# Two of four batches mixed as one 2x2 block product of seven products, with feature-major outputs

## The chip, the cores and the metric

The kernel runs on one core of one Trainium2 chip. The metric is the device time of one execution, in microseconds (us). Three runs of the kernel before took 250.44, 250.61 and 252.2 us; the median is 250.61. A profiled execution is a run of its own, whose span the views of the trace show.

## The reference

Polynomial-sketch attention for 4 batches of 4 heads, 1088 positions and 32 features a head, followed by a token-mixing block whose two 1088x1088 weight matrices are shared by all batches. The parts that matter here:

```
phi(x) = outer(S1 x, S2 x)                    # 8 x 8 sketch features
kv  = sum_s phi(k) v ;  z = sum_s phi(k)
x   = (phi(q) kv) / (phi(q) z + 1e-6)         # (4, 4, 1088, 32) -> (4, 1088, 128)
theta = x @ w_theta
zr, zi = x * cos(theta), x * sin(theta)
y   = einsum('ts,bsd->btd', w_tok_r, zr) + einsum('ts,bsd->btd', w_tok_i, zi)
u   = x + y
out = u + relu(u @ w_ch)                      # (4, 1088, 128), float32
```

The inputs `w_tok_r`, `w_tok_i`, `w_theta`, `w_ch`, `S1` and `S2` arrive as 64-bit floats and are turned into 32-bit floats by the kernel.

## The kernel before

The kernel is a list of operations, each recorded with its engine, an assumed duration, the buffers that it reads and writes, and a due time. The class `Layout` lays them out: a list scheduler with a duration model (`dve`, `act`, `pool_`, `LAT`) plays the engines forward and takes at each step the operation with the lowest rank; ranks come from due times, and the table `SHIFT` moves each stage's rank by a hand-held number. The order that comes out is what is issued on each engine (`issue`), and semaphores are set by the tile framework. Where the model sees a gap on TensorE in the first part, `issue` puts filler matmuls (`spin`, L432). Buffers come from pools by class: 22 of `big` (1152 floats a partition), 5 of `zs`, 6 of `g1`, 8 PSUM banks `ps`, and so on. Helpers issue nearly everything, so many groups of the profile share a line: `tt` is L380 (tensor_tensor, on DVE or POOL, and a custom DVE addition too), `ts` L384, `stt` L387, `mm` L400, and `join` L394 is a DMA issued by POOL that adds its source to its destination.

The stages, in their rough order of time:

- Keys and values of batch 0 are loaded and k is transposed (L789), sketched and summed into `kv`; then batch 1; then batches 2 and 3 together (`CHAINS`). q is loaded for each batch (L667 issues these loads on SP), transposed, and made into the levels `lv`.
- The mixing weights arrive as 17 rows of 1088 64-bit numbers a partition (`w_tok` into `zs`): 8 chunks of 128 source positions for the real matrix, 8 for the imaginary one, and one that holds the last 64 positions of both. A 64-bit row becomes a 32-bit one with two ACT operations (L651, L653), a DVE shift (L384) and a custom DVE addition (L380); it stays in a `big` buffer, `rows[i]`, with 128 source positions on partitions and 1088 target positions along the free axis.
- `outputs_x(b)` makes, in three groups of 384 positions, the attention's output `xT[b]` with features on partitions (ACT copy), theta, its cosine and sine, and `zt[b]`: 17 chunks of 128 positions by 128 features, the chunks of `x cos` first, then those of `x sin`, and the mixed one of 64 + 64.
- `mix_row(b, i, ...)` multiplies chunk i of `zt[b]` (standing, 128x128) with row i (moving, 384, 384 and 320 columns). 17 of these add up in PSUM to y of the batch, with features on partitions. Batch 0 does its three groups of columns together, row by row as the rows arrive; the later batches do one group after another. Batch 3 has other cuts (`LAST`: 320, 384, 256 and 128 columns), so that the last group is short.
- `mix_out(b, span, yp)` finishes a group of columns. For batches 0 and 1 (`UDMA`, `ODMA`), ACT copies y out of PSUM, and a `join` adds x; then for each 128 positions a matmul gives u @ w_ch with positions on partitions (u standing), a transpose gives u itself (L1168), ACT applies relu (L1183) and copies u (L1189), a second `join` adds them. For batches 2 and 3 both additions are DVE operations (L380) that read PSUM. The store (L1195, on SP) writes 512-byte rows.

All weight rows are kept until the end, since every batch needs them.

Of the kernel before, what the change touches and what calls it, by code (L numbers as in the profile page):

```python
# [22 lines left out]
P = 128  # L23
# [11 lines left out]
    "blocks_k": 73.9, "blocks_m": 29.8, "blocks_t": -262.8, "chain0": -12.2, "chain1": -7.3, "chain2": 57.8,  # L35
    "den0": -124.6, "den1": -153.1, "den2": 103.7, "den3": 241.9, "first": -48.4, "grid0": -93.7, "grid1": 2.6,
    "grid2": -78.4, "grid3": 13.5, "kT0": -128.1, "kT1": -103.7, "kT2": -37.4, "kT3": -24.2, "keys0": -394.4,
    "keys1": -128.6, "keys2": -52.3, "keys3": -193.5, "kf0": -216.8, "kf1": 19.7, "kf2": -83.1, "kf3": -91.6,
    "kv0": -174.5, "kv1": 35.5, "kv2": 8.3, "kv3": -25.5, "kvb0": 0.1, "kvb1": -229.1, "kvb2": 126.9,
    "levels0": -99.2, "levels1": -206.9, "levels2": 66.3, "levels3": 253.2, "loadh1": -83.9, "loadh2": -39.6,  # L40
    "loadh3": -67.9, "loadk0": 62.2, "loadk1": -58.1, "loadk2": -68.8, "loadk3": -79.3, "loadq0": -44.5,
    "loadq1": -58.0, "loadq2": -25.3, "loadq3": 17.3, "loadv0": -23.7, "loadv1": -50.2, "loadv2": -36.8,
    "loadv3": -35.8, "mix0_0": 247.6, "mix1_0": 81.4, "mix1_1": 70.9, "mix1_2": 137.9, "mix2_0": 319.4,
    "mix2_1": 370.4, "mix2_2": 512.5, "mix3_0": 275.2, "mix3_1": 124.7, "mix3_2": 81.7, "mix3_3": 52.5,
    "num0_0": -23.5, "num0_1": -122.6, "num0_2": -2.3, "num1_0": -980.1, "num1_1": -572.2, "num1_2": -805.8,
    "num2_0": 92.7, "num2_1": 137.9, "num2_2": 336.8, "num3_0": 216.9, "num3_1": 198.2, "num3_2": 256.2,
    "out0_0": 119.7, "out0_1": 79.8, "out0_2": 119.8, "out1_0": 206.2, "out1_1": 67.6, "out1_2": 380.5,
    "out2_0": 219.3, "out2_1": 329.6, "out2_2": 151.1, "out3_0": 206.6, "out3_1": 598.8, "out3_2": 247.9,
    "out3_3": 65.4, "q00": -178.0, "q01": -9.8, "q02": 44.9, "q03": 187.8, "qT0": -24.9, "qT1": 80.4, "qT2": 33.8,
    "qT3": 94.6, "qscale0": -72.3, "qscale1": 1.7, "qscale2": -12.0, "qscale3": 148.3, "rest0": -152.2,  # L50
    "rest1": -19.2, "rest2": 49.7, "rest3": -17.9, "row0": -3.7, "row1": -2.9, "row10": 57.0, "row11": 37.7,
    "row12": 37.2, "row13": 55.0, "row14": 73.7, "row15": 77.2, "row16": 66.5, "row2": 8.2, "row3": 28.3,
    "row4": 28.5, "row5": 29.4, "row6": 32.2, "row7": 33.8, "row8": 56.5, "row9": 60.6, "scaled": -81.5,
    "sliced": 215.7, "small": -186.7, "square2": -114.8, "sums0": -154.7, "sums1": -29.3, "sums2": 301.1,
    "sums3": -87.5, "theta0_0": -468.7, "theta0_1": -402.8, "theta0_2": -418.4, "theta1_0": -695.8,
    "theta1_1": -466.0, "theta1_2": -397.2, "theta2_0": 97.6, "theta2_1": 129.7, "theta2_2": 231.5,
    "theta3_0": 395.1, "theta3_1": 390.2, "theta3_2": 276.6, "w2": -38.6,
# [9 lines left out]
LAST = (0, 320, 704, 960)  # L67
# [4 lines left out]
ODMA = (True, True, False, False)  # L72
# [21 lines left out]
class Layout:  # L94
# [4 lines left out]
    LAT = {"P": 0.16, "V": 0.12, "A": 0.12, "G": 0.16, "S": 0.10}  # L99
# [58 lines left out]
    def lag(self, o, t):  # L158
        return o.fly + (0.0 if o.eng == t.eng else self.LAT[o.eng])

# [9 lines left out]
    def forward(self):  # L170
# [7 lines left out]
        channel = 0.0  # L178
# [51 lines left out]
        while done < len(ops):  # L230
# [12 lines left out]
            if e == "S":  # L243
                free[e] = t + self.ISSUE * max(o.lk, 1)
                channel = max(channel, free[e]) + o.dur
                o.end = channel + 2.0
            else:
                d = o.dur
                if e == "V" and o.lk > 1 and port["G"][1] > t - 0.3:
                    d += 0.25 * o.lk  # L250
                free[e] = t + d
                o.end = t + d + o.fly
                if o.lk and e in "VG":
                    port[e] = (t, t + d, o.lk)
# [9 lines left out]
            for s in o.succ:  # L264
                x = ops[s]
                x.wait -= 1
                x.ready = max(x.ready, o.end + (0.0 if x.eng == e else self.LAT[e]))
# [51 lines left out]
def kernel(  # L319
# [24 lines left out]
    GW = GC * P  # L344

# [46 lines left out]
    def join(dst, src, w, r, fly=ADD_FLY):  # L392

        op("G", 0.7, lambda: G.dma_start(dst(), src(), accum_op=ALU.add), w, r, fly=fly)  # L394
# [140 lines left out]
    op("G", 0.6, rests, [sf, sq], [sc, s0], lk=3)  # L535
# [61 lines left out]
    op("G", 1.9, lambda: blocks_m(0), [(mv[0], "s"), (mf[0], "s")], [s0, c16, cf, hm], lk=8)  # L597
# [233 lines left out]
    def chain(bs):  # L831
# [91 lines left out]
        op("G", 0.5 * nb, whole, [(mf[b], "y") for b in bs], [w_[1]] + [(mv[b], "y") for b in bs], lk=2 * nb)  # L923
        nus[bs] = nu

    def chain_out(bs):
        nu = nus[bs]
        at("kvb", bs[0])
        for n, b in enumerate(bs):
# [7 lines left out]
            op("G", 0.4, masks, [(mk, 0)], [bdm, nu, ec], lk=2)  # L937
# [7 lines left out]
            op("G", 0.6, eps, [(mk, 1), (qsb, 1)], [nu, (qsb, 0), ec], lk=3)  # L945
# [9 lines left out]
    qs, qx, q0, xT, zt = {}, {}, {}, {}, {}  # L955

# [95 lines left out]
    def outputs_x(b, lv, pool_qp):  # L1052
# [3 lines left out]
        for g in range(NG):  # L1056
# [32 lines left out]
            op("A", act(GW), lambda g=g, xp=xp: A.copy(xt()[:, g * GW:(g + 1) * GW], xp()), [(xt, g)], [xp])  # L1089
# [3 lines left out]
            cs = buf("g3", (2, GC, P), F32, "cs")  # L1093

            def turn(g=g, x=x, th=th):
                for i in range(GC):
                    y_ = xt()[:, g * GW + i * P:g * GW + (i + 1) * P]
                    T.transpose(x()[:, i], y_, ident())  # L1098

            def theta(g=g, th=th):  # L1100
# [4 lines left out]
            op("P", 0.67, theta, [th], [(xt, g), w2], hold=[cs])  # L1105
            op("P", 0.33, turn, [x], [(xt, g)])
# [12 lines left out]
                bc(x()[:, 0:full], 1, [P, 2, full, P]), cs()[:, :, 0:full], ALU.mult), [(z, g)], [x, cs])  # L1119
# [6 lines left out]


    rows = []

    def zkey(i):  # L1130
        return NG if i == NK - 1 else (i % NF) // GC

    def mix_row(b, i, gs, yps, due):
# [8 lines left out]
        op("P", w * 4 / 2400 + 0.01, f, yps, [(z, zkey(i)), rows[i]], due)  # L1142

    def mix_out(b, span, yp, due):
# [4 lines left out]
        xkeys = [(xt, j) for j in range(t0 // GW, (t1 - 1) // GW + 1)]  # L1149
        uT = buf("g1", (GW,), F32, "uT")  # L1150
        if UDMA[b]:
            op("A", act(w), lambda: A.copy(uT()[:, :w], yp()[:, :w]), [uT], [yp])
            join(lambda: uT()[:, :w], lambda: xt()[:, t0:t1], [uT], xkeys, ADD_FLY2)
        else:
            vop(w, lambda: tt(V, uT()[:, :w], xt()[:, t0:t1], yp()[:, :w], ALU.add), [uT], xkeys + [yp])
        po, un = buf("ps", (GW,), F32, "po"), buf("ps", (GW,), F32, "un")
        ot = buf("g1", (GC, DM), F32, "ot")
        nch = (w + P - 1) // P

        def lin():  # L1160
            for i in range(nch):
                sz = min(P, w - i * P)
                mm(po()[:sz, i * P:(i + 1) * P], uT()[:, i * P:i * P + sz], w2()[:, 1], True, True)

        def back():
            for i in range(nch):
                sz = min(P, w - i * P)
                T.transpose(un()[:sz, i * P:(i + 1) * P], uT()[:, i * P:i * P + sz], ident())  # L1168
# [121 lines left out]
```

## Time and profile before

| what | value |
|---|---|
| runs | 250.44, 250.61, 252.2 us (median 250.61) |
| span of the profiled execution | 248.5 us, 3915 instructions |
| TensorE (PE) busy | 239.7 us, 96%, 1480 matmuls |
| VectorE (DVE) busy | 142.1 us, 57%, 295 instructions |
| ScalarE (ACT) busy | 127.8 us, 51%, 255 |
| GpSimd (POOL) busy | 41.2 us, 17%, 96 |
| DMA | 34.54 MB in 11,922 packets, 139 GB/s on average; 2.23 MB of it written |
| granted TensorE clock | full, but for 0.94 of it in the stretch from 40 to 60 us |
| first product step of batch 0 (`mix_row`) | 63.67 us |

The profiled execution's span stands 2.1 us under the median of the runs. In the page's list of groups, each row names line, engine, operation, tiles and shapes, then the busy time of the group and the mean of one in ns, and at the end the idle time of the engine just before these instructions and what ended it. A matmul of 32-bit floats leaves two matmul records, and each record is about as long as its pipeline, longer than the distance between two starts; so a step is read as the distance from one start to the next. In a timeline, neighbouring instructions of one kind are drawn together, with their count behind the x.

### The profile page before, as it was taken

The page shows a single profiled execution, that of the slowest core. Times are in us where ns is not written, and L with a number is a line of the kernel's source. Part 1 is how long each engine was busy: PE and PEld are TensorE (multiplying, and loading weights), DVE is VectorE, ACT ScalarE, POOL GpSimd, SP SyncE. Part 2 cuts the span into 40 slices and gives each one's busy share as a digit, 9 for nine tenths or more (in the row PEclk, how much of TensorE's full clock was granted, in tenths as well). Part 3 has the DMA queues.
Part 4 walks back from the last instruction along what each step waited for, and adds up shares of the span by engine and source line. Part 5 has one row for each costly group of instructions (what it writes and reads, how often), then busy time and mean ns, then how long its engine had stood idle before and what let it go on. Part 6 is the DMA issues. An engine that isn't in the chain of part 4 may idle for free.

```text
span 248.5 us, 3915 instructions
## 1 busy us (share of the span) xinstructions
PE 239.7 (96%) x1480; PEld 178.6 (72%) x1480; DVE 142.1 (57%) x295; ACT 127.8 (51%) x255; POOL 41.2 (17%) x96
## 2 busy tenths in 40 slices
PE   7898999988999999999999999999999999999993
PEld 4797999958665766865766777696646679856773
DVE  2767898889988899999578101448802350100022
ACT  3787787589797998870433425674243360000011
POOL 1259441020000100007302332412000000000000
PEclk9999999997999999999999999999999999999999
DMA  6999999602470359991003255431101010000012
GB/s 204 372 417 338 423 369 427 282 0 95 154 291 3 96 175 356 370 396 57 3 0 63 63 92 127 79 66 24 30 0 34 0 32 3 0 11 0 0 47 59
DMA packets 11922, 34.54 MB, mean 139 GB/s; under 512 B 1280, under 2 KB 7296, under 8 KB 9728
## 3 DMA queue, kind: packets, MB, share of 16 engines
q1 hardware_dynamic: 9488, 30.29, 32.4%
q0 software_dynamic: 2320, 4.00, 8.2%
q8 instruction: 11, 0.18, 0.3%
q14 instruction: 7, 0.06, 0.1%
q10 hardware_dynamic: 96, 0.01, 0.0%
HBM read 28.07 MB, written 2.23 MB: 122 GB/s over the span
## 4 chain that ended last, share of the span: by engine, by line
PE 84%; DMA 11%; ACT 3%; SPq 0%; DVE 0%; issue 0%; DVEq 0%; ACTq 0%
PE ps L400 76%; DMA zs<-w_tok 6%; DMA big<-k_l 5%; PE ps L1076 3%; PE ps L1168 2%; PE ps L1098 2%; PE ps L987 1%; ACT big L651 0%; SPq L667 0%; ACT big L653 0%; PE ps L789 0%; ACT g L1111 0%; DVE g L387 0%; ACT g L1110 0%; ACT g L1107 0%
## 5 line engine op out<-in xcount | busy, mean ns | idle before, releaser
L400 PE MATMUL ps<-big,zs 128*128 128x384 f32 (+3 forms) x442 | 132.0, 447 | 0.0
L400 PEld LDWEIGHTS ps<-big,zs 128*128 128x128 f32 x442 | 78.2, 190 | 37.7 <-issue 2.6
L380 DVE CUSTOM_DVE_ANT_0 big<-big,big 128x2176 uint16<-128x2176 uint16 x17 | 21.9, 1291 | 3.4 <-ACT big L653 2.3
L651 ACT ACTIVATE big<-zs 128x1088 f32<-128x1088 f32 x17 | 20.7, 1219 | 4.8 <-DMA zs<-w_tok 4.8
L653 ACT ACTIVATE big<-zs 128x1088 int32<-128x1088 uint32 (+1 forms) x18 | 21.2, 1179 | 0.0
L380 DVE TENSOR_TENSOR g<-big,ps 128x384 f32<-128x384 f32 (+3 forms) x7 | 3.3, 478 | 26.8 <-PE ps L400 26.7
L1179 ACT COPY g<-ps 128x128 f32<-128x128 f32 (+1 forms) x2 | 0.6, 320 | 32.8 <-PE ps L1168 32.8
L1080 ACT COPY g<-ps 128x384 f32<-128x384 f32 x24 | 11.0, 487 | 11.1 <-PE ps L1076 11.0
L380 DVE TENSOR_TENSOR zs<-ps,g 128x768 f32<-128x768 f32 (+2 forms) x20 | 12.1, 627 | 7.4 <-ACT g L1113 5.7
L400 PE MATMUL ps<-mf,big 128*128 128x96 f32 x72 | 15.5, 313 | 0.0
L1183 ACT ACTIVATE g<-ps 128x384 f32<-128x384 f32 (+2 forms) x15 | 5.6, 401 | 18.7 <-PE ps L400 13.5
L387 DVE SCALAR_TENSOR_TENSOR g<-g,ps 128x384 f32<-128x384 f32 x12 | 6.6, 552 | 14.8 <-ACT g L1107 14.7
L384 DVE TENSOR_SCALAR big<-big 128x1088 int32<-128x1088 int32 x17 | 12.2, 719 | 1.8 <-ACT big L651 1.8
L400 PEld LDWEIGHTS <-hf 128*128 128x128 f16 (+1 forms) x144 | 11.9, 110 | 1.7 <-issue 1.3
L1020 ACT COPY lv<-ps 128x480 f32<-128x480 f32 x12 | 6.4, 578 | 12.3 <-PE ps L400 12.2
L400 PEld LDWEIGHTS ps<-w,big 128*128 128x128 f32 x72 | 9.3, 191 | 3.7 <-ACT big L1089 2.0
L400 PEld LDWEIGHTS ps<-mf,big 128*128 128x128 f32 x72 | 11.8, 207 | 0.0
L400 PE MATMUL ps<-w,big 128*128 128x128 f32 x72 | 10.0, 278 | 1.8 <-ACT big L1089 1.8
L380 DVE TENSOR_TENSOR g<-lv 128x768 f32<-128x768 f32 x12 | 11.1, 953 | 1.0 <-PE ps L1076 0.9
L1076 PEld LDWEIGHTS ps<-ident,g 128*128 128x128 f32 x72 | 8.7, 142 | 4.1 <-issue 1.3
L400 PE MATMUL ps<-mv,hf 128*128 128x96 f16 x108 | 11.2, 215 | 0.0
L1076 PE MATMUL ps<-ident,g 128*128 128x128 f32 x72 | 10.9, 275 | 0.0
(177 smaller groups left out, 371.5 us busy)
## 6 DMA issues: line engine op xcount, KB each, us to landing
zs<-w_tok SPq DMA_DIRECT2D x17, 1088.0 KB, 7.3
big<-k_l SPq DMA_DIRECT2D x7, 576.0 KB, 7.0
big<-q_l SPq DMA_DIRECT2D x4, 576.0 KB, 7.6
big<-v_l SPq DMA_DIRECT2D x4, 576.0 KB, 10.4
big<-hf POOLq DMA_DIRECT2D x3, 576.0 KB, 9.3
out<-g SPq DMA_DIRECT2D x7, 192.0 KB, 2.0
g<-big POOLq DMA_DIRECT2D x4, 192.0 KB, 2.9
g<-g POOLq DMA_DIRECT2D x4, 192.0 KB, 3.2
```

What stands on the lines that cost most here:

```text
L380: eng.tensor_tensor(out=o, in0=a, in1=b, op=f)
L384: (eng or V).tensor_scalar(out=o, in0=a, scalar1=s1, scalar2=s2, op0=op0, **kw)
L387: (eng or V).scalar_tensor_tensor(out=o, in0=a, scalar=s, in1=b, op0=op0, op1=op1)
L400: T.matmul(o, lhs, rhs, start=start, stop=stop, skip_group_check=True)
L651: op("A", 0.22 + n * 0.0009, lambda: A.activation(dfn(), words_of(raw(), n)[1].bitcast(F32), AF.Prelu, scale=2.0**-112, alpha=-(2.0**32)), ...
L653: op("A", 0.22 + n * 0.0009, lambda: A.activation(stp(), words_of(raw(), n)[0].bitcast(U32), AF.Copy, scale=2.0**-29), [stp], [raw])
L1020: op("A", act(480), lambda g=g, lp=lp: A.copy(lv().rearrange("p l (c n) -> p l c n", n=HR)[:, :, g * GC:(g + 1) * GC], lp().rearrange("p c ...
L1076: T.transpose(tr()[:, i * P:(i + 1) * P], qp()[:, i * H + 2 * n:i * H + 2 * n + 2].rearrange("p h i j -> p (h i j)"), ident())
L1080: op("A", act(GW), lambda n=n, tr=tr, qT=qT: A.copy(qT()[:, n], tr()), [(qT, n)], [tr])
L1098: T.transpose(x()[:, i], y_, ident())
L1168: T.transpose(un()[:sz, i * P:(i + 1) * P], uT()[:, i * P:i * P + sz], ident())
L1183: op("A", act(m), lambda n=n, i0=i0, i1=i1, o=o: A.activation(o(), po()[:n, i0 * P:i1 * P], AF.Relu), [(ot, j)], [po])
```

## The change

Batches 2 and 3 (`PAIR`) no longer run through `mix_row`. The two are one product: a 2x2 block matrix of z (rows: batch p = 2 and q = 3; columns: the 8 chunks of `x cos` and the 8 of `x sin`) times a 2x2 block matrix of weights (rows: real and imaginary; columns: the first and the second 544 target positions, `HT`). With a11 and a12 the first 544 columns of the real and of the imaginary rows, and a21 and a22 their second 544, `winograd` computes it in the variant of Strassen's algorithm with seven products in place of eight: each has 8 chunks and 544 columns, in two parts of 288 and 256 (`PARTS`). The sums of weights are made in place on the halves of the rows, "1" and "2" on DVE, "4" and "3" on POOL (`APOOL`); the sums of z (`zsub`) on DVE. Products accumulate on one another in PSUM where a later result contains an earlier one (`fresh=False`), and DVE adds each to `xT`, which becomes u. The mixed chunk of 64 + 64 positions is outside the block product and runs as single matmuls (`ends`).

Because sums of batches 2 and 3 are formed, batch 3 is scaled first by a power of two for each feature (`balance`): DVE takes the largest magnitude of each feature of x in both batches (two reductions over 1152 columns) and makes the factor in five small operations; ACT multiplies x by it (`xs`) ahead of the transposes, and the factor's inverse is applied when a product of batch 3 is added.

The outputs of all batches stay feature-major (`finish`): one matmul for a group of columns with `w_ch` standing and u moving, one DVE operation for relu and addition, a DVE transpose of 32x32 blocks, and four stores (one for each 32 features) in pieces of 128 bytes. `ODMA`, `LAST`, the transposes on TensorE (L1168) and the ACT operations of the old ending fall away. For batches 0 and 1 the `join` that adds x to y stays.

The order is laid out anew: the duration model has other constants, and every number of `SHIFT` is another. Dependencies on `xT`, `zt` and the rows are held in smaller pieces.

```diff
 SHIFT = {
...
 }
-LAST = (0, 320, 704, 960)
+PAIR = (2, 3)
+PARTS = ((0, 288), (288, 544))
+APOOL = ("4", "3")
-ODMA = (True, True, False, False)
...
-    LAT = {"P": 0.16, "V": 0.12, "A": 0.12, "G": 0.16, "S": 0.10}
+    LAT = {"P": 0.2, "V": 0.04, "A": 0.04, "G": 0.06, "S": 0.10}
+    SAME = {"P": 0.0, "V": 0.035, "A": 0.035, "G": 0.05, "S": 0.0}
+    OVER = {"P": 0.0, "V": 0.08, "A": 0.1, "G": 0.0, "S": 0.0}
+    WAKE = 0.25
...
+    HT = S // 2
+    SQ = 32
...
+            if src is not xt:
+                xs = buf("g1", (GW,), F32, "xs")
+                op("A", act(GW), lambda g=g, xs=xs: A.mul(xs(), xt()[:, g * GW:(g + 1) * GW], even()[:, 4:5]), [xs],
+                   cells(xt, g * GW, (g + 1) * GW) + [even])
...
+    def balance():
+        at("even")
+        for j, b in enumerate(PAIR):
+            vop(NC * P, lambda j=j, b=b: V.tensor_reduce(out=even()[:, j:j + 1], in_=xT[b](), axis=AX.X, op=ALU.max,
+                                                         apply_absolute_value=True), [(even, j)], [xT[b]])
+
+        def ratio():
+            e = even()
+            ts(e[:, 0:2], e[:, 0:2], TINY, ALU.max, 1.0 / TINY, ALU.min)
...
+            stt(e[:, 5:6], e[:, 1:2], 0.5, e[:, 2:3], ALU.mult, ALU.mult)
...
     def mix_out(b, span, yp, due):
...
-        def back():
-            for i in range(nch):
-                sz = min(P, w - i * P)
-                T.transpose(un()[:sz, i * P:(i + 1) * P], uT()[:, i * P:i * P + sz], ident())
...
+        finish(b, t0, w, u, [uT], due)
+
+    def finish(b, t0, w, u, keys, due):
+        po = buf("ps", (GW,), F32, "po")
+        ot = buf("g1", (GW,), F32, "ot")
+        op("P", w * 4 / 2400 + 0.01, lambda: mm(po()[:, :w], w2()[:, 1], u(), True, True), [po], keys + [w2], hold=[ot])
+        vop(w, lambda: stt(u(), po()[:, :w], 0.0, u(), ALU.max, ALU.add), keys, [po])
+        vop(w, lambda: V.transpose(out=ot()[:, :w], in_=u()), [ot], keys)
+
+        def store():
+            for f in range(DM // SQ):
+                SY.dma_start(out[b, t0:t0 + w, f * SQ:(f + 1) * SQ].rearrange("(c j) i -> j c i", j=SQ),
+                             ot()[f * SQ:(f + 1) * SQ, :w].rearrange("j (c i) -> j c i", i=SQ))
+
+        op("S", w * P * 4 / 100e3, store, [], [ot], due, lk=4)
+
+    def winograd(t):
...
+        def asum(name, dst, x, y, f):
+            at("ac", name)
+            E, e = (G, "G") if name in APOOL else (V, "V")
+            for i in range(NF):
+                op(e, pool_(HT) if e == "G" else dve(HT), lambda i=i: tt(E, dst[0](i), x[0](i), y[0](i), f), [dst[1](i)],
+                   [x[1](i), y[1](i)], lk=1)
...
+        def add(b, h, j, ps):
+            c0, c1 = (x + h * HT for x in PARTS[j])
+            u = lambda: xT[b]()[:, c0:c1]
+            k_ = cells(xT[b], c0, c1)
+            if b == p:
+                vop(c1 - c0, lambda: tt(V, u(), u(), ps()[:, :c1 - c0], ALU.add), k_, [ps])
+            else:
+                vop(c1 - c0, lambda: stt(u(), ps()[:, :c1 - c0], even()[:, 5:6], u(), ALU.mult, ALU.add), k_, [ps, even])
...
+        product("1", bx, re_p, a11, [(p, 0)])
+        product("2", two("pz"), im_p, a12, [(p, 0)], (p, 0))
+        done(p, 0)
+        zsub("1", t1, re_q, re_p)
+        asum("1", a21, a21, a22, ALU.add)
+        product("5", by, t1, a21, [(q, 1)])
+        zsub("2", t2, im_q, t1)
+        asum("2", a21, a21, a11, ALU.subtract)
+        product("6", bx, t2, a21, [(q, 0)], fresh=False)
+        asum("4", a12, a12, a21, ALU.subtract)
+        product("3", by, im_q, a12, [(q, 0)], (q, 0), fresh=False)
+        done(q, 0)
...
+        zsub("3", re_q, im_q, re_q)
+        asum("3", a21, a22, a21, ALU.subtract)
+        product("7", bx, re_q, a21, [(q, 1)], fresh=False)
+        done(q, 1)
+        zsub("4", im_p, im_p, t2)
+        product("4", bx, im_p, a22, [(p, 1)], (p, 1), fresh=False)
+        done(p, 1)
```

Where the cut of the diff hides a line: the seven products are `product(name, banks, zz, aa, sinks, extra, fresh)`, 8 matmuls for each of the two parts, then the `ends` of the 64 + 64 positions if `extra` is given, and an `add` for each entry of `sinks`. In the code, `quarter(0, 0)` is a11, `quarter(1, 0)` a12, `quarter(0, 1)` a21 and `quarter(1, 1)` a22.

## The prediction

> **What bounds the kernel now.** I read the first lines of the page, then its slices, the groups, and the last microseconds of the timeline.
>
> ```profile
> span 248.5 us, 3915 instructions
> PE 239.7 (96%) x1480; PEld 178.6 (72%) x1480; DVE 142.1 (57%) x295; ACT 127.8 (51%) x255; POOL 41.2 (17%) x96
> PE   7898999988999999999999999999999999999993
> DVE  2767898889988899999578101448802350100022
> POOL 1259441020000100007302332412000000000000
> PE 84%; DMA 11%; ACT 3%; SPq 0%; DVE 0%; issue 0%; DVEq 0%; ACTq 0%
> L400 PE MATMUL ps<-big,zs 128*128 128x384 f32 (+3 forms) x442 | 132.0, 447 | 0.0
> ```
>
> TensorE is busy 96% of the span, and 84% of the chain that ended last is its own work. DVE's average, 57%, hides two stages: it is full until slice 19 (about 120 us) and nearly idle after slice 26. So a saving of TensorE work is worth its full time late, and in the first half only where DVE keeps up. The windows (PE, PEld, DVE, ACT, POOL busy, then clock) show that stage:
>
> ```profile
> 60.00:80.00 20.00, 20.00 (x117) 13.50 (x117) 18.06 (x28) 16.37 (x27) 0.00 (x0) 0.97 0.47 168
> 80.00:100.00 20.00, 20.00 (x104) 13.72 (x102) 18.43 (x27) 17.76 (x26) 0.93 (x1) 1.00 0.61 202
> 100.00:120.00 20.00, 20.00 (x144) 14.49 (x141) 18.86 (x39) 9.41 (x12) 6.73 (x9) 1.00 0.63 250
> 120.00:140.00 20.00, 20.00 (x101) 13.81 (x101) 11.24 (x18) 8.60 (x14) 3.27 (x6) 1.00 0.15 26
> ```
>
> The end, and the price of product steps, in the timeline (start, length, engine, line, tile, count, idle time before):
>
> ```profile
> 216.46 11.13 PE L400 MATMUL ps<-big,zs 128*128 128x384 f32 x34
> 227.69 7.70 PE L400 MATMUL ps<-big,zs 128*128 128x320 f32 x28
> ...
> 242.30 0.83 PE L400 MATMUL ps<-w,g 128*128 128x128 f32 x6
> ...
> 244.19 0.55 PE L1168 MATMUL ps<-ident,g 128*128 128x128 f32 x3
> 244.30 0.54 ACT L1183 ACTIVATE g<-ps 128x256 f32<-128x256 f32 x2 [0.65 <-PE ps L400]
> 244.85 0.61 DVE L380 TENSOR_TENSOR g<-g,ps 128x256 f32<-128x256 f32 x2 [0.61 <-ACT g L1183]
> ```
>
> One f32 matmul is two records. A 384-column record takes one step of 0.323 us (11.13 us for 34, less the length that overlaps the next), a 320-column one 0.269, a 128-column one 0.11. That is 1.68 ns per column of an f32 matmul, in every width.
>
> **TensorE's work.** Before, batches 2 and 3 cost 2 x 17 rows x 1088 = 36,992 columns, 62.2 us. After: seven products of 8 chunks x 544 columns, and four separate steps of 544 for the odd 64 rows, 32,640 columns, 54.8 us. Change −7.3. The outputs before: 36 blocks, each a 128x128 linear matmul (2 x 0.11) and a transpose (0.11), 12.0 us. After: 4352 columns with the weight standing, 7.3 us, no transposes: −4.7. The order of both kernels' instructions shows three more filler matmuls (`spin`); they run where TensorE would wait: 0.
>
> **The tail.** Before, the last transpose's record starts at 244.47 and is done one step later, 244.58; from there to the end of the span, 248.52, are 3.94 us. After, the last product is followed by a DVE add (256 columns: 0.42 by a row of that size at L380, and with the handovers 0.75 in which TensorE idles), the linear matmul (its 0.43 is counted above), the relu-and-add (0.42), a 32x32-block transpose on DVE, and four store issues on SP where the last group had two. A DVE transpose is not in the trace: bounds 0.30 (DVE's 128-column rows) and 0.82 (twice the 256-column row); I take 0.42, since it reads and writes as much. Store issues stand 0.43 apart, so the last comes 1.3 us after the first; then 1.8 us to land (1.5 to 2.0 in the trace) and 0.95 us from landing to the end, as now. 0.75 + 0.42 + 0.42 + 0.2 (two handovers) + 1.3 + 1.8 + 0.95 = 5.84 against 3.94: +1.9 (+1.2 to +3.0).
>
> **DVE in the stage from 60 to 120 us.** The sums for two of the seven products (8 + 8 tensor_tensor of 544) and the subtractions of z (12 of 256 or 384 columns), 16 relu or transpose operations of outputs in place of fewer, add about 30 us of DVE work, 142 to 172. ACT loses 6. Most of the added work stands behind 120 us where DVE is busy 21.6 of 60 us: hidden there. But with the orders of both kernels priced by the trace's rows, the first product step comes after 62.9 us of TensorE's work (52.8 before) and 60.5 us of DVE's (48.9 before). From there to the matmul of the last weight row TensorE has 40.6 us of work and DVE 39.3, mostly unpacking of weight rows:
>
> ```profile
> L380 DVE CUSTOM_DVE_ANT_0 big<-big,big 128x2176 uint16<-128x2176 uint16 x17 | 21.9, 1291 | 3.4 <-ACT big L653 2.3
> L384 DVE TENSOR_SCALAR big<-big 128x1088 int32<-128x1088 int32 x17 | 12.2, 719 | 1.8 <-ACT big L651 1.8
> ```
>
> DVE was busy 55.35 of the 60 us up to 120: 92%. At 92% its 39.3 us need 42.7, 2.1 longer than TensorE's 40.6. I take +2.0; bounds 0 (gaps close, for the rows wait less when DVE is ahead) and +4.7 (the gap of those 60 us falls on TensorE whole). In `SP`'s queue the load of batch 3's q now follows two stores of batch 0 (eight issues at about 0.45 = 3.6 us); it took 7.6 us to land, and by the order of work it has about 2 us to spare: 0 to +1.6, taken 0.
>
> **The chain of the block product.** Each sum of weights must be ready before the product that reads it. TensorE eats one 544-column row in 0.91 us. Eight rows of two sums (`APOOL`: "4" and "3") are made on POOL. No POOL operation of that size is in the trace; the slope has to come from small ones, and the risk from what they do beside DVE:
>
> ```profile
> L380 POOL TENSOR_TENSOR pbd<-psc,hm 128x128 f32<-128x128 f32 x2 | 0.8, 400 | 0.2
> L380 POOL TENSOR_TENSOR sbk<-s,hm 128x64 f32<-128x64 f32 x1 | 0.3, 293 | 0.1
> 116.14 1.96 POOL L384 TENSOR_SCALAR sm<-sm,qs 128x4 f32<-128x4 f32 x1
> 118.07 0.20 POOL L380 TENSOR_TENSOR sm<-sm,bdm 128x4 f32<-128x4 f32 x1
> 118.36 1.79 POOL L384 TENSOR_SCALAR sm<-sm,ec 128x4 f32<-128x4 f32 x1
> ```
>
> 128 columns take 0.400 and 64 take 0.293 us: 1.67 ns per column, so 544 take about 1.09. A floor is DVE's own 0.72 (its rows of 384 and 576 give 0.55 and 0.76), a ceiling 2.4: 1.09 plus a blocked wait as long as the 1.3 us that the rows at 116 and 118 lost (1.96 and 1.79 against 0.2 to 0.6). Counted in TensorE's own work along the order, the first row can be begun at 180.3 us and the last is needed at 211.0: 30.7 us; 16 x 1.09 = 17.4 plus about 5 us lost beside DVE operations fit. Per row POOL is slower than TensorE (1.09 against 0.91), so only the last rows of the first sum can slip: 0 to 1. The scaling of batch 3 (two DVE reductions over 1152 columns, about 1.27 each, five small operations 0.9, ACT copies 0.5 each) makes a chain of 3.7 us with 4.0 us of TensorE work beside it; if that cover is gone, it costs 3.7. The subtractions of z may slip 0.5. I take +1.2 for all; 0 to +6.
>
> The Trainium skill ("SBUF — State Buffer", section "Who interferes with whom") says that a DVE instruction with two inputs in SBUF and a GpSimd instruction that reads SBUF shut each other out for a whole instruction. The stretched rows at 116 and 118 us agree, and the rule speaks against sums on POOL. Its page "GPSIMD Engine Reference" (section "3.1 Elementwise — side-by-side cycle accounting") gives 4497 ns for 2048 f32 elements, an estimate of 1.2 us for 544, and by it the sum would rise by about 0.5.
>
> **The stores.** 17 become 56, of 128-byte pieces: 2.23 MB make 17,408 pieces. The trace's packets took 13 ns (128 bytes) to 27 ns (512), so 14 to 29 us per engine of 16, spread over the 120 us behind the first outputs, in which the DMA engines are busy half of the time at most. SP issues 56 x 0.45 = 25 us, also spread. Both hidden; without it, only the tail's share above.
>
> **The front.** Everything before 60 us is laid anew. TensorE idles there about 10.8 us now, most of it waiting for k and weights at the start. I see no reason for a gain or loss in work: 0, bounds −3 to +3.
>
> **Sum.** 248.5 − 7.3 − 4.7 + 1.9 (tail) + 2.0 (DVE) + 1.2 (chain) + 0 = 241.6 us of span. The runs are 250.44, 250.61 and 252.2; their median is 2.1 above the span. Predicted: 241.6 + 2.1 = 243.7.
>
> **Rivals.**
> A. The waits stay hidden: DVE +0.5, chain +0.3, front −1 in place of +2.0, +1.2 and 0: 240.3. For it: DVE is idle after 140 us, and the order of work is free to fill gaps. Against: 92% of DVE in the middle. Chance 0.27.
> B. DVE bounds the stage to 120 us: it loses the full 4.7, and the front 1 more: 243.7 + 2.7 + 1 = 247.4. For it: a later first product means that all rows are unpacked against less TensorE work. Against: ACT is relieved, so DVE waits less. Chance 0.18.
> C. POOL decides. With 2.4 us for a sum, 16 take 38 us where 30.7 are there. Up to about 1.6 us each ((30.7 − 5) / 16) the order hides them; beyond that each 0.1 us costs 1.6 us: 8 x 1.6 = 12.8, less the 1.2 counted: 255.3, slower than before. It decides from there on, and at about 2.1 us a sum the gain is gone. For it: POOL's stretched rows. Against: DVE is idle most of the time there, and most of its late operations read one operand from PSUM. Chance 0.07.
> The block product doesn't save: if each 288- or 256-column step cost as much as a 384-column one, its saving would be lost; but 256- and 320-column steps in this trace follow the 1.68 ns. I give no chance of its own.
>
> **How the numbers follow.** The sum as above has 0.48; its own range is 241.5 to 246. To hold 8 in 10 the range goes down past A (239.0) and up past B (248.5); outside stay C and the ends of A and B. This kernel's measurement can tell about 1% from no change: faster means below 248.1, slower above 253.1. Faster: A, the sum and most of B, 0.86. Same: the rest of B and a mild C, 0.07. Slower: C and a stalled front, 0.07.
>
> **What would show it.** Right: TensorE's product steps of 0.43 and 0.48 us (256 and 288 columns) add up to about 55 us for the last two batches; outputs have no records of L1168; POOL's sums take 1.0 to 1.3 us; TensorE's idle time between 60 us and the end is 2 to 5 us, with DVE (weight rows) as releaser in the first half and POOL or DVE (sums) in the second; the last matmul ends about 5 us ahead of the end. Wrong: TensorE waits of over 5 us before the product that reads sum "4", POOL sums near 2 us, a first product later than 74 us (63.7 now, plus the 10.1 us of work moved ahead of it), or a fall of the granted clock, which here dropped to 0.94 between 40 and 60 us after a wait of 2 us.

## The result, and the profile after

The changed kernel takes 242.53 us (median; 240.43 to 246.28) where the kernel before took 250.56: a ratio of 0.9645, 95% interval 0.9577 to 0.9712. (The ratio goes by the fast runs alone: it leaves out the execution of 246.28 us, which ran in a slower state.) Taken again later (the run "again" below) it took 241.3 us, ratio 0.9636 (0.9609 to 0.9664). The forecast was 243.7 us, with 239.0 to 248.5 as its range.

Its executions differ with the clock that TensorE was granted: the one of 246.28 us has a mean clock of 0.962, the one of 240.43 has 0.992. The first profile is of the longest one (span 244.5 us), so the lines below come from a second profile of the same kernel (span 240.0, clock 0.979), but for the clock line of the first, which is needed further down. The page of the second:

```profile
span 240.0 us, 3846 instructions
PE 228.8 (95%) x1405; PEld 176.0 (73%) x1405; DVE 181.7 (76%) x358; ACT 120.1 (50%) x233; POOL 55.5 (23%) x104
PE   7898899999999999999999999999999998999991
DVE  3598979999999999998589946497248899553441
PEclk9979799999999999999999999999999999999997
```

and the clock line of the first:

```profile
PEclk9989558999999999999999999999999999999998
```

TensorE is as full as before, with 11 us less of it. DVE has 40 us more, and is now busy in the second half as well; the forecast had about 30 us more. Three points of the trace cut the time into parts (the first product step; the start of the last matmul's last record; the end of the span):

| us | before | changed, first profile | changed, second profile |
|---|---|---|---|
| first product step | 63.67 | 78.42 | 73.96 |
| from there to the last matmul | 180.80 | 160.71 | 160.72 |
| from there to the end | 4.05 | 5.37 | 5.36 |
| span | 248.5 | 244.5 | 240.0 |

Everything behind the first product step is the same to 0.01 us in both profiles, 18.8 us less than before. The work that the new order puts ahead of that step is in the first row: about 9.0 us, counted in the two traces as what TensorE's steps other than products and outputs lost behind it (41.3 us before, 32.4 after). What differs between the two profiles lies in the first row alone, so the other two are the ruler by which the experiments are read.

The windows of the second profile (PE, PEld, DVE, ACT, POOL, clock):

```profile
60.00:80.00 20.00, 19.76 (x160) 15.12 (x157) 19.57 (x31) 19.85 (x36) 0.92 (x3) 1.00 0.54 201
80.00:100.00 20.00, 20.00 (x83) 12.78 (x81) 19.38 (x35) 13.39 (x17) 0.00 (x0) 1.00 0.59 224
100.00:110.00 10.00, 10.00 (x49) 7.10 (x48) 9.83 (x15) 9.78 (x17) 0.00 (x0) 1.00 0.33 112
```

DVE is busy 98% of these 50 us where it was busy 92% of its stage before, and TensorE lost 0.24 us. The one longer wait behind the first product step is in the block product:

```profile
201.42 2.77 PE L416 MATMUL ps<-big,zs 128*128 128x288 f32 x11 [1.01 <-DVE big L403]
```

The tail, in the timeline:

```profile
231.74 2.11 PE L416 MATMUL ps<-big,zs 128*128 128x256 f32 x9
233.88 0.42 DVE L396 TENSOR_TENSOR big<-big,ps 128x256 f32<-128x256 f32 x1 [2.05 <-PE ps L416]
234.36 0.70 PE L416 MATMUL ps<-big,w 128*128 128x256 f32 x2 [0.51 <-DVE big L396]
235.10 0.42 DVE L403 SCALAR_TENSOR_TENSOR big<-ps,big 128x256 f32<-128x256 f32 x1 [0.79 <-PE ps L416]
235.56 0.45 DVE L1217 STREAM_TRANSPOSE g<-big 128x256 f32<-128x256 f32 x1
```

The last step of the linear matmul ends at 234.90 (0.215 behind its last start), and 5.14 us follow it: two DVE operations, four stores issued one by one, the landing.

### The profile page after: what moved, and what is told of

It is laid out like the page before. It is cut to its first block, busy times and chain, and to the rows that moved or that the text cites. A ratio compares the mean times of both kernels' runs of the same rounds, so it can differ in the third digit from the quotient of the medians.

```text
span 244.5 us, 3846 instructions
## 1 busy us (share of the span) xinstructions
PE 233.3 (95%) x1405; PEld 180.2 (74%) x1405; DVE 182.0 (74%) x358; ACT 120.0 (49%) x233; POOL 55.5 (23%) x104
## 4 chain that ended last, share of the span: by engine, by line
PE 79%; DVE 9%; ACT 6%; DMA 2%; issue 1%; SPq 1%; DVEq 0%; ACTq 0%
PE ps L416 72%; DVE big L396 3%; PE ps L1096 3%; DMA big<-k_l 2%; DVE zs L396 2%; ACT big L669 2%; PE ps L805 2%; DVE sm L403 1%; PE ps L1007 1%; PE ps L1129 1%; ACT g L1100 1%; ACT big L667 1%; DVE big L403 1%; ACT big L705 1%; ACT big L1109 1%
## 5 line engine op out<-in xcount | busy, mean ns | idle before, releaser
L416 PE MATMUL ps<-big,zs 128*128 128x384 f32 (+3 forms) x380 | 110.5, 436 | 1.2 <-DVE big L403 1.0
L416 PEld LDWEIGHTS ps<-big,zs 128*128 128x128 f32 x380 | 69.7, 190 | 30.6 <-issue 5.0
L416 PE MATMUL ps<-big,big 128*128 128x128 f32 (+2 forms) x136 | 29.6, 356 | 0.0
L410 POOL DMA_DIRECT2D g<-big x6 | 5.4, 1008 | 105.8 <-PE ps L1096 55.8
L396 POOL TENSOR_TENSOR big<-big,big 128x544 f32<-128x544 f32 x16 | 23.4, 1488 | 20.1 <-DVE big L396 14.7
L416 PEld LDWEIGHTS ps<-big,big 128*128 128x128 f32 x136 | 23.2, 210 | 3.8 <-issue 0.9
L1206 ACT COPY g<-ps 128x384 f32<-128x384 f32 (+1 forms) x6 | 2.7, 470 | 42.0 <-PE ps L416 41.9
L1100 ACT COPY g<-ps 128x384 f32<-128x384 f32 x24 | 10.4, 485 | 14.3 <-PE ps L1096 14.2
L396 DVE TENSOR_TENSOR big<-big,hf 128x1152 f32<-128x1152 f32 x8 | 10.9, 1368 | 0.1
L416 PE MATMUL ps<-g,big 128*64 128x128 f32 x144 | 11.0, 304 | 0.0
L416 PE MATMUL ps<-sbk,g 128*128 128x64 f32 x72 | 10.9, 302 | 0.0
```

The costliest lines, as they stand in the source:

```text
L396: eng.tensor_tensor(out=o, in0=a, in1=b, op=f)
L410: op("G", 0.9, lambda: G.dma_start(dst(), src(), accum_op=ALU.add), w, r, fly=fly)
L416: T.matmul(o, lhs, rhs, start=start, stop=stop, skip_group_check=True)
L1100: op("A", act(GW), lambda n=n, tr=tr, qT=qT: A.copy(qT()[:, n], tr()), [(qT, n)], [tr])
L1206: op("A", act(w), lambda: A.copy(u(), yp()[:, :w]), [uT], [yp])
```

## The experiments

Where a run keeps "the order", every operation that it shares with the changed kernel stands at the same place of its engine's queue.

**again.** No edit.

> The changed kernel unaltered, to see what of its time is the same in every execution. In its first profile TensorE waited 2.06 us at 22.8 us and the granted clock was 0.50 from 25 to 37 us. Theory 1 (the drop of the clock follows that wait, and the wait's length varies): executions between 240 and 246.5 us, mean clock 0.96 to 0.99, the longer ones with the lower clock; behind 70 us the trace is the same to 0.5 us. Theory 2 (the spread comes from the block product's waits on POOL): the clock is alike and the waits behind 180 us differ by several us.

Measured: 241.3 us (240.53 to 241.95), the middle part 160.72 against 160.71. Theory 1 holds in that the waits of the block product are the same, 1.01 us in all behind 180 us, and what differs is the front. It does not hold in that the wait's length makes the difference: the wait is 2.06 us in both profiles. The chain, in the timeline of the second profile:

```profile
21.71 2.72 DVE L403 SCALAR_TENSOR_TENSOR sm<-sm,kg,g 128x128 f32<-128x128 f32 x1
25.07 1.04 PE L416 MATMUL ps<-sbt,sm 128*128 128x64 f32 x4 [2.06 <-ACT sm L862]
```

and the window behind it, with the clock third from the end:

```profile
25.00:30.00 5.00, 4.93 (x45) 4.70 (x45) 4.57 (x10) 2.66 (x9) 0.02 (x1) 0.66 1.05 381
```

A DVE operation on 128x128 that took 0.35 us in the kernel before takes 2.72; TensorE waits 2.06 us for what follows it; about 2 us behind the wait's beginning the clock falls to 0.50. It stayed there for 3.4 us in this execution and for 13.7 (24.7 to 38.4 us) in the first, which is the longer dip in the two clock lines above; why it lasted longer is not shown. Both executions have another fall of 3.4 us at about 11 us, behind waits of 0.74 and 0.56 us.

The longer the clock was down ahead of the first product step, the later that step came, over all executions profiled whose front is the changed kernel's own: 71.1 to 71.8 us with no fall (plain8, oldout2, poolsums), 72.7 with 3.4 us (dvesums), 74.0 to 74.2 with 6.8 (again, twoq, oldout), 78.4 with 17.1 (the first profile).

**plain8.** Eight ordinary products, the order kept.

```diff
-        zsub("1", t1, re_q, re_p)
-        asum("1", a21, a21, a22, ALU.add)
-        product("5", by, t1, a21, [(q, 1)])
+        product("5", by, re_q, a21, [(q, 1)])
...
+        product("8", by, re_p, a21, [(p, 1)])
-        product("4", bx, im_p, a22, [(p, 1)], (p, 1), fresh=False)
+        product("4", bx, im_p, a22, [(p, 1)], (p, 1))
```

> The changed kernel with eight ordinary products in place of seven: no sums of weights and no differences of z; scaling, feature-major outputs and the order of everything else as in the changed kernel. Theory (the saved product is worth its steps, 8 x 544 x 1.68 ns = 7.3 us, less the 1.0 us wait for a late addition): 6.3 us longer than the changed kernel, 247 to 250. Rival (the sums, their waits and POOL's lock take most of the saving back): at most 3 us longer, 243 to 246.

Measured: 246.75 us (ratio to before 0.9859, 0.9795 to 0.9924), the middle of two executions of 245.3 at a clock of 0.996 and two of 248.1 and 248.6 at 0.979. The middle part is 167.03 us, with the tail 172.39 against 166.08: +6.31, the 6.3 expected; the rival, at most 3, is refuted. The seven products save 6.9 us of steps (126.3 against 119.4 from start to start, all batches) and cost 0.7 more of waits (1.01 against 0.30).

**oldout and oldout2.** Outputs as before: linear matmuls with u standing, transposes on TensorE, relu on ACT, an addition on DVE, 512-byte stores; the order of all else kept.

```diff
-        op("P", ..., lambda: mm(po()[:, :w], w2()[:, 1], u(), True, True), ...)
-        vop(w, lambda: stt(u(), po()[:, :w], 0.0, u(), ALU.max, ALU.add), keys, [po])
-        vop(w, lambda: V.transpose(out=ot()[:, :w], in_=u()), [ot], keys)
+        for f, d, o, h in ((lin, 0.223, po, [ot]), (back, 0.11, un, [])):
+            op("P", d * nch, f, [o], keys + [w2], hold=h)
...
```

> The changed kernel with the outputs of before: blocks of 128 positions with u standing, transposes on TensorE, relu on ACT, one addition on DVE, 512-byte stores. Order of all else as in the changed kernel. Theory: TensorE has 38 blocks x 0.332 = 12.6 us in place of 7.3, the tail is 1.8 us shorter: 3.5 us longer than the changed kernel, 244.5 to 248. Rival (DVE's transposes and the short stores cost as much as TensorE saves): within 1 us.

Measured: 269.74 us, which says nothing of the outputs. My order had put the transposes at the first place where their input is issued, ahead of the products; TensorE takes its queue in turn and waited 11.9 us in four places for the accumulating DMA, and the clock fell to 0.50 at each of the four.

> As the run before with the outputs of before, but each group's transposes stand behind its linear matmuls in TensorE's queue (in that run they stood ahead of them, at once behind the accumulating DMA, and TensorE waited 11.9 us for it in four places; it said nothing of the outputs). Theory: TensorE 38 blocks x 0.332 = 12.6 us in place of 7.3, the tail 1.3 to 1.8 us shorter: 3.5 to 4 us longer than the changed kernel, 244 to 247. Rival (DVE's transposes and the 128-byte stores cost as much as TensorE saves): within 1 us of it, 240.5 to 242.5.

Measured: 246.36 us (0.9806, 0.9732 to 0.988). Middle part 167.77 (+7.06), tail 4.03 (−1.33): together +5.72, more than I expected. The difference is in the steps: the outputs' TensorE steps add up to 14.3 us, not 12.6, against 7.5 in the changed kernel. Full blocks take 0.12 us a step from start to start, not 0.11, and the 32-wide blocks that cuts at 288 columns leave take 0.17 in their linear matmuls. These 6.9 us are nearly all of the 7.06, so the rival is refuted: no cost of DVE's transposes and the short stores shows but the tail's 1.3 us.

**dvesums.** The sums "4" and "3" on DVE.

```diff
-                op(e, ..., lambda i=i: tt(E, dst[0](i), x[0](i), y[0](i), f), [dst[1](i)],
+                op(e, ..., lambda i=i: tt(V, dst[0](i), x[0](i), y[0](i), f), [dst[1](i)],
```

> The changed kernel with the sums "4" and "3" issued on DVE, at the places that they had in the order; nothing on POOL between 185 and 225 us. Theory (POOL's sums lock DVE: its 0.42 to 0.72 us operations took 1.4 to 1.9 us eight times between 190 and 212, and TensorE's 1.01 us wait at 204.9 is for one of DVE's late additions): DVE's operations keep their 0.42 to 0.72, 16 more of 0.63 stand in DVE's idle time, the wait goes: 1.0 us less than the changed kernel from the first product to the end (166.1 to 165.1). Rival (DVE is too full there, so the wait grows): 1 to 4 us more.

Measured: 242.19 us, the middle part with the tail 167.52 against 166.08: +1.44. Half of the theory holds: without POOL's sums the DVE operations that had taken 1.4 to 1.9 us there (six, not eight) take their 0.42 to 0.72 us again. The other half fell: the 16 more operations fill DVE, and TensorE waits 0.42, 0.73, 0.35 and 0.16 us in place of 1.01 once. The rival was right: in this order POOL is the better place for these sums, though it stretches DVE's operations.

**poolsums.** All 32 sums on POOL (`tt(G, ...)` in the same line).

> The changed kernel with the sums "1" and "2" on POOL too, at the places that they had in the order: all 32 sums of 544 columns on POOL, none on DVE. Theory (the forecast's third rival, at its price: POOL takes 1.33 us a sum alone and up to 1.8 beside DVE; 32 x 1.45 = 46 us where about 32 are there, from 185 to 222): TensorE waits 10 to 18 us for sums, 251 to 259 us in all, slower than or level with the kernel before. Rival (the order hides it): within 3 us of the changed kernel.

Measured: 250.57 us in the profiled execution, and 254.64 to 256.59 in three others, at clocks of 0.956 to 0.969 (0.987 in the first). Middle part with tail 177.06: +11.0. In its waits:

```profile
PE ps L416 <- POOL big L396: 4.0, 5, 1.5
PE ps L1096 <- DVE g L396: 3.8, 1, 3.8
```

and its timeline:

```profile
132.87 6.21 DVE L396 TENSOR_TENSOR g<-lv 128x768 f32<-128x768 f32 x2
134.03 4.22 POOL L396 TENSOR_TENSOR big<-big,big 128x544 f32<-128x544 f32 x3
```

4.0 us of waits are for sums, where I expected 10 to 18. As much again was for something that I had not expected: two DVE operations that take 0.95 each took 6.21, for the second ended only 0.8 us behind the end of a row of three sums; it was out for the whole row, not for one sum's 1.4 us. The half clock that followed (139.8 to 143.2) took some more. So the third rival is real, though not by the price of a sum (1.47 us in the mean here, 1.49 in the changed kernel): with twice as many sums on POOL the change brings nothing.

**rowdup.** One more DVE operation for each weight row.

```diff
-        op("V", n * 0.00053 + 0.15, lambda: ts(dfn().bitcast(I32), dfn().bitcast(I32), 3, ALU.logical_shift_left),
+        op("V", n * 0.00053 + 0.15, lambda: [ts(dfn().bitcast(I32), dfn().bitcast(I32), m_, ALU.logical_shift_left) for m_ in (2, 1)],
```

> The changed kernel with the DVE shift of each weight row made in two steps (by 2 and by 1 in place of 3): one more DVE operation of 0.72 us for each of 17 rows, 12.2 us with its handover, 11 of them (7.9 us) behind the first product step. It tells how much room DVE has up to 110 us, where the prediction saw a loss of 2.0 us and the trace shows TensorE waiting 0.19. Theory (DVE is busy 98% there and just keeps up): 9 to 12 us longer, TensorE waiting for rows. Rival (DVE could still have taken several us): at most 6 longer.

Measured: 252.0 us, 10.7 more than "again", in the theory's 9 to 12. The middle part is 168.10: of 7.9 us added there, 7.4 arrive. DVE has half a microsecond of room in that stage. The window that had lost 0.24 us loses 2.85:

```profile
60.00:80.00 20.00, 17.15 (x146) 13.43 (x145) 19.66 (x28) 16.10 (x32) 0.00 (x0) 1.00 0.48 174
```

**late.** Nine small POOL copies moved behind POOL's work for batch 0.

```diff
+        late = [o for o in self.order if o.stage == "blocks_m" and o.lk == 3]
...
+            if o.stage == "chain0" and o.eng == "G":
+                seq += held
+                held = []
```

> The changed kernel with nine small copies on POOL (27 to 31 of its instructions, 22.2 to 24.0 us) moved behind POOL's work for batch 0, nothing else. Theory (DVE's 128x128 operation of 2.72 us at 21.49 stood behind POOL's unbroken row of small instructions; TensorE's wait of 2.06 us follows, and the half clock from 25 to 37 us follows that): that operation takes under 1 us, TensorE's wait is under 0.7 us, the clock is 1.00 from 20 to 40, 238 to 240.5 us. Rival (the drop of the clock has another cause): the wait goes, the clock still falls, time as the changed kernel's.

Measured: 240.75 us (0.9612, 0.9596 to 0.9628), which the spread of "again" does not tell from no change. In the profiled execution DVE's operation takes 0.46 us, and TensorE's wait for it is gone; but TensorE goes no further than the next late input:

```profile
19.88 0.46 DVE L415 SCALAR_TENSOR_TENSOR sm<-sm,kg,g 128x128 f32<-128x128 f32 x1
28.38 1.22 PE L428 MATMUL ps<-big,big 128*128 128x128 f32 x4 [2.28 <-DMA big<-hf]
```

The accumulating DMA of batch 1's k, issued at 18.45, needs 9.9 us to land while the DMA engines are full of weight rows. TensorE waits 2.28 us for it, and the clock is 0.50 from 27 to 34: one wait took the other's place.

That the moved copies did it is not shown. The same operation took 0.45 to 0.49 us in plain8, oldout, oldout2, dvesums, poolsums and twoq as well, where the copies stand as in the changed kernel, and TensorE's wait was for the DMA there too. In plain8:

```profile
20.15 0.49 DVE L420 SCALAR_TENSOR_TENSOR sm<-sm,kg,g 128x128 f32<-128x128 f32 x1
28.26 0.71 PE L433 MATMUL ps<-big,big 128*128 128x128 f32 x4 [1.72 <-DMA big<-hf]
```

So whether DVE is late there differs from one execution to the next. With the copies in their place and the front unaltered, it was late in the two executions in which the clock had already fallen at 11 us: there the operation starts at 21.5 and 21.7 us, in the six others at 20.1 to 20.4. Whether this start is the cause is not tested, and it is not the whole of it: in late_fill, below, the operation starts at 20.1 and is late all the same.

**late_fill.** As late, with 11 filler matmuls ahead of the matmul that waits for that DMA.

```diff
+                if o.stage == "rest1" and late:
+                    late = []
+                    for _ in range(11):
+                        fill()
```

> As the run with the nine POOL copies moved back (there TensorE's wait moved on to the accumulating DMA of batch 1's k, 2.28 us at 26.1, and the clock was 0.50 from 27 to 33), with 11 more filler matmuls (1.8 us) ahead of the matmul that waits for that DMA. The wait itself stays. Theory (the clock falls only where TensorE is without work for more than about 1.75 us, and the executions differ by how long it stays down): clock 1.00 from 15 us to the end of the products, first product step at 71 to 71.8 us where it was 73.7, 238 to 239.5 us in all, executions within 1 us. Rival (the clock falls for other reasons): 240.5 to 242, spread as before.

Measured: 239.19 us (238.89 to 240.35), ratio 0.9532 (0.945 to 0.9613). First product step at 71.62; the clock is 1.00 up to the tail:

```profile
25.00:30.00 5.00, 5.00 (x47) 4.35 (x45) 3.46 (x12) 2.37 (x6) 1.08 (x3) 1.00 1.05 391
```

Three of four executions have mean clocks of 0.992 or more, one 0.985. The same DVE operation had again been late in the profiled one, with the copies moved (1.91 us, and a wait of 1.17 us, with no fall of the clock). The fillers do not shorten an execution that keeps its clock: plain8 and oldout2 came to the first product step at 71.1 and 71.4 us without them. What they seem to do is to make such executions more frequent: the four of late, without fillers, had clocks of 0.983 to 0.991. On few executions this is likely, not shown.

**twoq.** The last four stores on two queues.

```diff
+                q_ = A if (b, t0 + w) == (PAIR[0], S) and f % 2 else SY
-                SY.dma_start(
+                q_.dma_start(
```

> The changed kernel with the last group's four stores issued on SP and ACT in turn, two each. Theory (the tail holds three issue steps of 0.49 us between the first and the last store): two steps fewer, 5.37 us from the last matmul's start to the end of the span become 4.4, and the time 0.9 us less. Rival (the stores' landing sets the end, or ACT's issue is slower): within 0.2 us.

Measured: 241.29 us; from the last matmul to the end 4.91 in place of 5.37: −0.46, half of what I expected. The median is that of "again" (241.3). In the trace the last store is issued 0.92 us earlier behind the last matmul, as expected, but lands only 0.75 earlier (it takes 1.82 us from its issue on ACT, 1.66 on SP), and from the last landing to the end stand 1.32 us in place of 1.01. Why the end came later behind the landing is not shown.

**best2.** late_fill and twoq together.

> The run with the late POOL copies and 11 more filler matmuls, with the last four stores on SP and ACT in turn as well. Theory (the gains stand apart, one in the front and one in the tail): 0.46 us less than 239.2: 238.7, and 2.5 to 3.5 less than the changed kernel; from the first product step to the end 165.6 us. Rival: one undoes the other, 239.2 or more.

Measured: 238.67 us (238.25 to 238.97), ratio to before 0.9533 (0.9503 to 0.9563); first product step at 70.81, from there to the end 165.66. The two gains stand apart as expected, it beats both kernels, and its executions are within 0.8 us of one another.

**before_fill.** The kernel before, with ten fillers in its 1.76 us wait at 55 us.

```diff
             def theta(g=g, th=th):
+                for _ in range(10 * (b == 0 and g == 0)):
+                    T.matmul(th().rearrange("p c d -> p (c d)"), idle()[:, 0:P], idle(), start=True, stop=True, skip_group_check=True)
```

> The kernel before, with ten filler matmuls (1.6 us, on arrays of zeros, into the bank that the next matmul overwrites) in TensorE's wait of 1.76 us at 55.0 us, behind which the clock was 0.50 from 57.8 to 61.0. Theory (the wait lets the clock fall, in this kernel too): clock 1.00 at 57 to 61, the first product step 1.6 us earlier than 63.67, 248.6 to 249.3 us where the kernel before has 250.6. Rival (the clock falls whatever TensorE does there, or the fillers delay it): 250 to 251.

Measured: 250.71 us, ratio 1.0014 (0.9988 to 1.0039): nothing. In its profile the wait is filled, the fall of the clock at 57 to 61 us is gone, and the first product step comes at 62.45, 1.2 us earlier. But the clock fell at 11 to 15 us, behind waits of 0.56 and 0.67 us, and the middle part is 0.45 us longer. So filling this wait was worth nothing in the kernel before. What decides whether the clock falls behind such short waits stays open.

## Why the prediction was right, point by point

The sum was 241.6 us of span; the second profile has 240.0. By its terms:

| term | forecast | measured | by |
|---|---|---|---|
| products | −7.3 | −6.6 against the old ones; −6.9 against eight with the new cuts | steps of both kernels; plain8 |
| outputs, steps | −4.7 | −6.1 (13.5 to 7.5) | steps of both kernels |
| tail | +1.9 | 0.67 + 5.14 = 5.81 against 3.94: +1.9 | second profile |
| DVE to 120 us | +2.0 | +0.24 (waits of TensorE) | second profile, rowdup |
| waits of the block product | +1.2 | +1.01 | second profile, dvesums |
| front | 0 | +1.3; +5.8 in the first profile | first product step, less the 9.0 us of work moved ahead of it |

The balance, with TensorE's steps read from start to start: the middle part is 20.08 us shorter. Products give 6.6 of it (126.0 to 119.4, all batches), outputs 6.2 (6.1 with the very last step of each kernel, which stands behind that part), work moved ahead 9.0; waits that were not there before take 1.7 (0.19, 1.01 and the 0.51 ahead of the last linear matmul, which the table counts in the tail). The terms of the table add up to −8.3, 240.2 us, where 240.0 were measured.

So there is luck in the sum. It is right to 1.6 us while three of its terms are off by more than a microsecond: DVE's stage 1.8 too much, the outputs' saving 1.4 too little, the front 1.3 too little. The old outputs took 0.12 us a step in the trace, the 64-wide blocks 0.18 in their linear matmuls, where the forecast priced all at 0.11. The 2.1 us added for the runs were a little much as well: a run's time stands mostly 1.8 above its own span here.

**Mis-sized: DVE's stage.** The step most off is "at 92% its 39.3 us need 42.7". The bound of DVE was right in kind (rowdup: half a microsecond of room) but not its loss. From the first product step to the end of the last weight row's unpacking 39.3 us passed (73.96 to 113.22), with DVE busy 38.3 of them, or 98%, and TensorE waiting 0.19. The 92% was a property of the old order, and I carried it over as one of the engine.

**Right in sum, wrong in its parts: the waits of the block product.** The forecast priced a sum on POOL at 1.09 us from the slope between 64 and 128 columns. It takes 1.33 alone and 1.49 in the mean:

```profile
L396 POOL TENSOR_TENSOR big<-big,big 128x544 f32<-128x544 f32 x16 | 23.4, 1485 | 20.1 <-DVE big L396 14.7 <-PE ps L416 4.6 <-issue 0.7
```

It fits all the same, as the sum had 1.6 us of room for each. The 1.01 us wait is not for a sum: it is for DVE's addition of a product, behind a DVE operation that took 1.86 us beside POOL's sums where it takes 0.72 alone. The chain that scales batch 3 cost nothing; its cover held, for the scaled x is there by 183 us with no wait of TensorE. The Trainium skill's estimate ("GPSIMD Engine Reference", section "3.1 Elementwise — side-by-side cycle accounting"), 1.2 us, was nearer than mine, and still short of the 1.33. Its rule on the shared port ("SBUF — State Buffer", section "Who interferes with whom") agrees with DVE's stretched operations; but to leave POOL empty of sums, which one could take from it, costs 1.44 us more by dvesums.

**The front.** "I see no reason for a gain or loss" was within its bounds for the second profile and missed the spread. The 10.8 us that it reads as idle before are not mostly waiting for k and weights: the trace before has 5.1 us of idle time ahead of the first product step, 1.7 lost to a half clock, and 23 filler matmuls. The spread is the half clock (17.1 us of it in the first profile, 6.8 in the second, none in best2, which comes to the first product step 3.1 us earlier than the second). The forecast named the fall of the clock as a sign of being wrong, and a first product step later than 74 us as another: in the first profile both came, the step at 78.42. So whether the forecast of 0 for this stage fits depends on the execution that is looked at.

**Rivals.** A (240.3: waits stay hidden) is nearest for DVE's stage; its gain in the front came only in executions without a fall of the clock, as in best2. B (DVE loses its full 4.7) is refuted by the windows. C (POOL decides) is not this kernel, but poolsums shows it, 16 sums further. Four signs named at the end came out: product steps of 0.43 and 0.48 us (215 and 242 ns a record), no transposes in the outputs, the releaser of TensorE's waits being DVE, and a tail of 5 us; POOL's sums were over the 1.0 to 1.3 named, and TensorE's waits behind the first product step, 1.7 us up to the last matmul, under the 2 to 5.

## What to carry to other kernels

Where one engine is full, count its steps in both kernels by one price list: that forecast 12.0 us here where 12.7 were measured, and the tail to 0.1; read the price of a step from rows of the same kind and width. An engine's share of busy time can belong to its order, not to the engine: DVE's went from 92% to 98% here, so a loss carried over from the old order should be bounded from zero. Where a trace varies between executions, cut it at a fixed event: behind the first product step two executions 4.5 us apart agreed to 0.01 us, and most of what best2 gains lies ahead of it. And before a change is credited with what its profile shows, look whether executions without it show the same, as with late.

## What was not expected of the hardware

- A row of GpSimd operations without a break can keep a DVE operation with its operands in SBUF out until the row ends, not for one instruction only: 2.72 us against 0.35 beside small operations and copies that started 0.2 apart, and 6.21 for two against 1.9 beside three sums of 1.4. It need not: beside other unbroken rows of sums DVE came in after one sum (0.42 us became 1.4 to 1.6), and the 0.35 us operation took 0.45 to 0.49 in six executions with the same row. What decides is not shown.
- The clock of TensorE was halved for 3 to 14 us after waits of 1.66 (twoq) to 2.28 us (late) in the front, and stayed up after waits of 1.72 (plain8), 2.22 (oldout2), 2.25 (poolsums) and 2.37 us (rowdup) there. So a wait of about 2 us is a risk and not a rule. The Trainium skill ("TensorE: Matmul & The Clock Gate", section "HAM oscillation — how this bites in real kernels") puts the limit at idle gaps of about 3.4 us; here shorter gaps were enough at times, and the measurement decides.
- Within one execution the clock's changes stand whole multiples of 3.41 us apart: 11.07, 14.48, 24.73 and 38.38 us in the first profile, falls at 27.94, 120.10, 143.99, 188.37 and 253.22 in oldout. So a fall came 0.9 us (late) to 2.65 us (dvesums) behind the beginning of its wait. How a wait lies against these steps does not settle by itself whether the clock falls: in the 3.41 us ahead of the next step TensorE was busy 2.39 us in late, and the clock fell, and 1.55 us in rowdup, and it did not.
- The two waits in the front are one behind the other: where the first was gone (late, plain8, twoq), the second was 1.66 to 2.28 us long.
